# Seven half products for two of three output tiles: a float32 expert layer on one Trainium2 core

## The chip, the core and the metric

The kernel runs on one core of one Trainium2 chip. The metric is the device time of one execution, in microseconds. The profile names the engines PE (TensorE matmul), PEld (TensorE weight load), DVE (VectorE), ACT (ScalarE), POOL (GpSimd) and SP (SyncE).

## The reference

A recurrent attention block feeds a mixture of experts with a hierarchical gate; all inputs and outputs are float32.

```python
# attention: q, k, v, f_logit are (B, H, S, D) = (4, 8, 768, 48)
f = 1.0 / (1.0 + np.exp(-f_logit))
for t in range(S):
    state = f[:, :, t, :, None] * state + np.einsum('bhd,bhe->bhde', k[:, :, t], v[:, :, t])
    y[:, :, t] = np.einsum('bhd,bhde->bhe', q[:, :, t], state)
# x = y as (B*S, H*D) = (3072, 384); G = 4 groups of Eg = 4 experts, F = 1024
g_logits = x @ w_group;  g_idx = argmax(g_logits);  g_w = softmax(g_logits)[g_idx]
for g in range(G):
    xg = x[g_idx == g];  e_logits = xg @ w_expert[g]
    e_idx = argmax(e_logits);  e_w = softmax(e_logits)[e_idx]
    for e in range(Eg):
        h = np.maximum(xg[e_idx == e] @ w1[g, e], 0.0)       # (tokens, 384) @ (384, 1024)
        ye = h @ w2[g, e]                                    # (tokens, 1024) @ (1024, 384)
        out[rows of these tokens] = (g_w * e_w)[:, None] * ye
```

## The kernel before

The first part of the kernel computes attention in chunks of 128 tokens, routes every token to one of 16 experts, and writes the token rows to `x_dram` in DRAM, with the token's gate weight and number behind the 384 features. The experts are ranked by their number of tokens. The second part, which the change is about, runs sixteen expert passes, one for each entry of `PLACES`. Two experts have had their first 128 tokens computed early; what is left of them makes passes 0 and 15, of 128 columns. Passes 1 to 14 are wide: one expert each, with 230, 222, 214, 212, 208, 204, 200, 196, 193, 191, 189, 186, 182 and 174 columns (`WIDTHS`), one column for each token that the pass has room for.

A wide pass goes through these steps:

- `fetch` (L393): GpSimd gathers the token rows (`xg`) by an indirect DMA, three passes ahead. `load_weights` (L381) issues the DMAs of w1 and w2 on SyncE's queue, 1536 KB each, also three passes ahead, as buffers come free.
- `square_in` (L415): 16 transposes of VectorE turn the rows into features by tokens (`xe`). One such instruction turns 32x32 squares of 32 partitions, with 192 or 96 elements each, and writes them to the other 32 partitions where they belong.
- `up` (L439, L440): the first layer. 8 output tiles of 128 features, three products each (a 128x128 block of w1 as the stationary operand, all tokens of the pass moving), two tiles to a PSUM bank, and ScalarE's Relu behind each of the four banks, into `h`.
- `down` (L475, L476): the second layer, turned: three output tiles `m` of 128 features, each the sum of 8 products in one bank (block of w2 stationary, `h` moving), copied by ScalarE into `yT`.
- `square_out` (L422): 16 transposes of VectorE turn `yT` back to token rows `yr`.
- `scaled` and `put` (L447, L450): ScalarE multiplies two blocks of rows by the gate weight into `yt`, and GpSimd scatters them to the output.

In float32 each product is two matmul instructions and two weight loads in the trace. `manual_schedule` holds TensorE, VectorE, ScalarE and SyncE to the order in which the program is written, so the order of the loop is the order of each engine's queue. Iteration n of the loop writes: `square_out` of pass n-1, `square_in` of pass n+2, `up` of pass n+1, `scaled` of pass n-1, `down` of pass n, and the weight loads of pass n+3. So the first layer of the next pass stands on TensorE before the second layer of this pass, and VectorE turns the last pass's output and a later pass's input beside it. In iteration 14 no first layer is left there; that of pass 15 comes after the loop, followed by `turn_out` of pass 14 (transposes on TensorE) and the row-wise second layer of pass 15 (`down_rows`, L460).

PSUM has eight banks in rotation (tag `bank`). After iteration 2, `beyond` computes a table on VectorE of what the passes had no room for (L340 to L372); after iteration 3, `weakest` and `flags` reduce the decays, with one transpose on TensorE (L869). With these inputs the branch that they decide is not taken.

Of the kernel before, what the change touches and what calls it, by code (L numbers as in the profile page):

```python
# [10 lines left out]
FP32 = mybir.dt.float32  # L11
# [4 lines left out]
OP = mybir.AluOpType  # L16
AX = mybir.AxisListType.X
ET = mybir.EngineType
P = 128
SQ = 32  # L20
# [3 lines left out]
def kernel(  # L24
# [12 lines left out]
    nc = tc.nc  # L37
    B, H, S, D = q.shape
    N, DM = out.shape
# [8 lines left out]
    KO = DM // P  # L48
    FO = F // P
    NL = G + GE  # L50
    WIDE = 2 * P
# [28 lines left out]
    def bank(shape, name):  # L80
        return ps.tile(shape, FP32, tag="bank", name=name)
# [253 lines left out]
    def beyond(all_, sb):  # L335

        def tmp(shape, name):
            return sb.tile(shape, FP32, tag=name, bufs=1, name=name)

        SHP = (P, NOV, GE)  # L340
        from_ = tmp([P, GE], "from")
        if all_:
            nc.vector.memset(from_, 0.0)
        else:
            wide = tmp([P, GE, GE], "wide")
            nc.vector.tensor_tensor(wide, order, own.unsqueeze(2).broadcast_to((P, GE, GE)), OP.mult)
            nc.vector.reduce_sum(out=from_, in_=wide.rearrange("p n e -> p e n"), axis=AX)
        nc.vector.tensor_tensor(from_, from_, base, OP.add)
        total = tmp([P, GE], "total")
        nc.vector.tensor_tensor(total, run, from_, OP.subtract)  # L350
        more = tmp([P, GE, NT], "more")
        nc.vector.tensor_tensor(more, total.unsqueeze(2).broadcast_to((P, GE, NT)), steps.unsqueeze(1).broadcast_to((P, GE, NT)), OP.is_gt)
        nb = tmp([P, GE], "nb")
        nc.vector.reduce_sum(out=nb, in_=more, axis=AX)
        end = tmp([P, GE], "end")
        nc.vector.tensor_tensor_scan(end, unit, nb, 0.0, OP.mult, OP.add)
        nc.vector.tensor_copy(b_end, end[0:1, GE - 1:GE])
        beg = tmp([P, GE], "beg")
        nc.vector.tensor_tensor(beg, end, nb, OP.subtract)
        bl = blocks.unsqueeze(2).broadcast_to(SHP)  # L360
        passed = tmp(list(SHP), "passed")
        nc.vector.tensor_tensor(passed, bl, end.unsqueeze(1).broadcast_to(SHP), OP.is_ge)
        be = tmp([P, NOV], "be")
        nc.vector.reduce_sum(out=be, in_=passed, axis=AX)
        nc.vector.tensor_scalar(b_expert, be[0:1], float(GE - 1), None, OP.min)
        mine = tmp(list(SHP), "minb")
        nc.vector.tensor_tensor(mine, bl, beg.unsqueeze(1).broadcast_to(SHP), OP.is_ge)
        nc.vector.tensor_tensor(mine, mine, passed, OP.subtract)
        off = tmp([P, GE], "off")
# [32 lines left out]
    def squares(w, turn):  # L402


        for k_ in range(P // SQ):
            n = sum(j * P + k_ * SQ < w["n"] for j, m in w["blocks"])
            for g in range(P // SQ):
                turn(n, k_, slice(k_ * SQ, (k_ + 1) * SQ), g, slice(g * SQ, (g + 1) * SQ))

    def square_in(w):  # L410

        w["xT"] = room(w, KO, "xe")
        x = w["x"][:, :, 0:DM].rearrange("p j (o g c) -> p j g o c", o=KO, c=SQ)
        xT = w["xT_full"].rearrange("p o (j k c) -> p j k o c", j=2, c=SQ)
        squares(w, lambda n, k_, rk, g, rg: nc.vector.transpose(out=xT[rg, 0:n, k_], in_=x[rk, 0:n, g]))  # L415

    def square_out(w):

        w["rows"] = w["pool"].tile([P, 2, DM], FP32, tag="yr", name="yr")
        y = w["rows"].rearrange("p j (o g c) -> p j g o c", o=KO, c=SQ)  # L420
        yT = w["yT_full"].rearrange("p o (j k c) -> p j k o c", j=2, c=SQ)
        squares(w, lambda n, k_, rk, g, rg: nc.vector.transpose(out=y[rk, 0:n, g], in_=yT[rg, 0:n, k_]))  # L422

    def turn_in(w):
        w["xT"] = room(w, KO, "xe")
# [6 lines left out]
    def up(w, w1):  # L432
        n = w["n"]
        w["h"] = h = room(w, FO, "h")
        for f in range(0, FO, 2):
            hp = bank([P, 2, n], "hp")
            for o in range(2):
                for ko in range(KO):
                    nc.tensor.matmul(hp[:, o, :], lhsT=w1[:, ko, (f + o) * P:(f + o + 1) * P], rhs=w["xT"][:, ko, :], start=(ko == 0), stop=(ko == KO - 1))  # L439
            nc.scalar.activation(h[:, f:f + 2, :], hp, AF.Relu)  # L440
            yield
# [14 lines left out]
    def down_rows(w, w2):  # L456

        yp = bank([P, DM], "yo")
        for fo in range(FO):
            nc.tensor.matmul(yp, lhsT=w["h"][:, fo, :], rhs=w2[:, fo, :], start=(fo == 0), stop=(fo == FO - 1))  # L460
            if fo == FO - 4:
                yield
        put(w, 0, P, yp)

    def down(w, w2):
        n = w["n"]
        if n == P:
            for _ in down_rows(w, w2):
                pass
            return  # L470
        w["yT"] = w["yT_full"][:, :, 0:n]
        for m in range(KO):
            yp = bank([P, n], "yo")
            for fo in range(FO):
                nc.tensor.matmul(yp, lhsT=w2[:, fo, m * P:(m + 1) * P], rhs=w["h"][:, fo, :], start=(fo == 0), stop=(fo == FO - 1))  # L475
            nc.scalar.copy(w["yT"][:, m, :], yp)  # L476

    def scaled(w, settle=False):
        if w["n"] > P:
# [39 lines left out]
    with ExitStack() as fast:  # L519
        sb = fast.enter_context(tc.tile_pool(name="sb", bufs=2))  # L520
        fp = fast.enter_context(tc.tile_pool(name="fp", bufs=1))

        def kept(shape, name):
            return fp.tile(shape, FP32, tag=name, name=name)
# [258 lines left out]
        first, routes = [], []  # L783
# [99 lines left out]
    ws = {n: pass_of(n) for n in range(3)}  # L883
    ahead = {n: load_weights(wq if n % 3 == 1 else wp, who[0:1, PLACES[n]:PLACES[n] + 1]) for n in range(1, 2)}
    ahead[0] = weights[0]

    def const_out(i):

        t = mo.tile([P, KO, WIDE], FP32, tag=f"yT{i}", bufs=1, name=f"yT{i}")
        nc.gpsimd.memset(t[:, :, P:WIDE], 0.0)  # L890
        return t

    def run_up(n):
        for _ in up(ws[n], ahead[n][0]):
            pass

    outs = [const_out(i) for i in range(2)]
    turn_in(ws[0])
    for _ in first[0]:
# [4 lines left out]
    turn_in(ws[1])  # L904
    for _ in opening:
        pass
    for n in range(GE - 1):
# [5 lines left out]
        past, coming = ws.pop(n - 1, None), ws.get(n + 2)  # L913
        if past and past["n"] > P:
            square_out(past)
        if coming and coming["n"] > P:
            square_in(coming)
        if n + 2 < GE:
            run_up(n + 1)
        if past:  # L920

            scaled(past, n == GE - 3)
        if coming and coming["n"] == P:
            turn_in(coming)
        w["yT_full"] = outs[n % 2]
        down(w, ahead.pop(n)[1])
        if n + 3 < GE:
            ahead[n + 3] = load_weights(wq if n % 3 == 1 else wp, who[0:1, PLACES[n + 3]:PLACES[n + 3] + 1])
        if n == 2:
            with tc.tile_pool(name="tb", bufs=1) as tb:  # L930
                beyond(False, tb)
        if n == 3:
            weakest()
            flags()

# [10 lines left out]
    def scan():  # L946

        sb = slow.enter_context(tc.tile_pool(name="sb2", bufs=2))
        y_dram = dp.tile([B * HP, S, 2 * D], FP32, name="y_dram")
        with tc.For_i(0, B * HP, 1) as i:  # L950
            tT = {}
            for nm, src in (("f", f_logit), ("q", q), ("k", k), ("v", v)):
                t = sb.tile([P, NC, 2, DP], FP32, tag="nat", name="nat")
# [15 lines left out]
            yp = [bank([P, HC, 2, D], "yp") for _ in range(2)]  # L969
# [19 lines left out]
        for c in range(NC):  # L989
            lgs = sb.tile([P, B, NL], FP32, tag="lgs2", name="lgs2")  # L990
            for b in range(B):
                x = sb.tile([P, HP, 2, DP], FP32, tag="x2", name="x2")
# [9 lines left out]
                xT = sb.tile([P, HP, P], FP32, tag="x2T", name="x2T")  # L1002
# [7 lines left out]
        beyond(True, sb)  # L1010


    more = nc.values_load(both[0:1, 1:2], min_val=0, max_val=1, skip_runtime_bounds_check_because="the result of a comparison")
    with tc.If(more > 0), ExitStack() as late:
# [3 lines left out]
        mo = late.enter_context(tc.tile_pool(name="mo2", bufs=2))  # L1018
        last = nc.values_load(b_end[0:1, 0:1], min_val=0, max_val=NOV, skip_runtime_bounds_check_because="a count of blocks that N bounds")
        with tc.For_i(0, last, 1) as i:  # L1020
            w1, w2 = load_weights(wp, b_expert[0:1, bass.ds(i, 1)])
# [4 lines left out]
            tb = bank([P, 2], "tb2")  # L1026
# [4 lines left out]
            ts = mo.tile([P, 2], FP32, tag="ts", name="ts")  # L1031
# [3 lines left out]
            w = fetch(ep, row, P, late=True)  # L1035
# [32 lines left out]
```

## Time and profile before

| what | value |
|---|---|
| median of 14 runs | 421.12 us (420.17 to 422.84) |
| the profiled execution | 421.87 us, of which the profile's span is 420.1 us |
| granted TensorE clock, mean | 0.994 |
| TensorE busy, weight loads busy | 408.9 us, 376.4 us |
| VectorE, ScalarE, GpSimd busy | 266.8, 156.8, 83.2 us |
| attention and routing | up to about 149 us of the span |
| passes 1 to 14 | 185 to 404 us of the span |
| second layer of the wide passes (L475) | 672 matmuls, 115.8 us busy |
| output transposes (L422) | 208 instructions, 70.5 us busy |

Busy time counts the time in which an engine had at least one instruction under way; a matmul's end is modelled, and matmuls overlap, so the time from one start to the next says more than one matmul's length. A row's last part names what ended the engine's idle time before it. Line numbers are those of the kernel before.

### The profile page before, as it was taken

The page shows a single profiled execution, that of the slowest core. Times are in us where ns is not written, and L with a number is a line of the kernel's source. Part 1 is how long each engine was busy: PE and PEld are TensorE (multiplying, and loading weights), DVE is VectorE, ACT ScalarE, POOL GpSimd, SP SyncE. Part 2 cuts the span into 40 slices and gives each one's busy share as a digit, 9 for nine tenths or more (in the row PEclk, how much of TensorE's full clock was granted, in tenths as well). Part 3 has the DMA queues.
Part 4 walks back from the last instruction along what each step waited for, and adds up shares of the span by engine and source line. Part 5 has one row for each costly group of instructions (what it writes and reads, how often), then busy time and mean ns, then how long its engine had stood idle before and what let it go on. Part 6 is the DMA issues. An engine that isn't in the chain of part 4 may idle for free.

```text
span 420.1 us, 10066 instructions
## 1 busy us (share of the span) xinstructions
PE 408.9 (97%) x4047; PEld 376.4 (90%) x4047; DVE 266.8 (64%) x778; ACT 156.8 (37%) x353; POOL 83.2 (20%) x127
## 2 busy tenths in 40 slices
PE   8999999999999998999999999999999999999995
PEld 3888888888877966879999999999999999999992
DVE  5666878788886810550599785495685695594240
ACT  6777776767554311211122122231231231231220
POOL 4000010101012166001021331312222221110230
PEclk9999999999999999899999999999999999999999
DMA  9999997878999469937548385595685785585010
GB/s 178 204 201 217 191 177 146 153 140 162 309 335 394 124 235 354 379 92 290 166 165 292 111 321 193 202 324 144 246 316 143 276 300 196 219 318 161 27 46 25
DMA packets 132145, 88.98 MB, mean 212 GB/s; under 512 B 102582, under 2 KB 122748, under 8 KB 132090
## 3 DMA queue, kind: packets, MB, share of 16 engines
q1 hardware_dynamic: 125666, 75.50, 61.7%
q0 software_dynamic: 5792, 11.92, 9.3%
q10 hardware_dynamic: 632, 0.83, 0.6%
q8 instruction: 34, 0.56, 0.5%
q14 instruction: 21, 0.17, 0.1%
HBM read 78.71 MB, written 9.83 MB: 211 GB/s over the span
## 4 chain that ended last, share of the span: by engine, by line
PE 47%; issue 30%; DMA 7%; POOL 6%; DVE 4%; another core or an unknown queue 2%; ACT 1%; POOLq 1%; DVEq 1%
PE hp L439 11%; PE yo L475 6%; DMA out_dram<-yt,xg 6%; PE ap L659 5%; PE y L701 5%; POOL out_dram L450 4%; PE cs L600 4%; PE yo L460 2%; PE x_ps L742 2%; POOL xg L393 2%; PE tr_k L634 2%; PE tr_q L634 2%; PE ds L676 2%; PE y L697 2%
## 5 line engine op out<-in xcount | busy, mean ns | idle before, releaser
L439 PE MATMUL hp<-xe,w 128*128 128x128 f32 (+14 forms) x864 | 141.3, 323 | 2.6 <-issue 1.9
L439 PEld LDWEIGHTS hp<-xe,w 128*128 128x128 f32 x864 | 137.5, 192 | 4.5 <-issue 2.5
L475 PE MATMUL yo<-h,w 128*128 128x230 f32 (+13 forms) x672 | 115.8, 333 | 0.0
L422 DVE STREAM_TRANSPOSE yr<-yT 32x192 f32<-32x192 f32 (+1 forms) x208 | 70.5, 339 | 70.4 <-ACT yT L476 67.8
L475 PEld LDWEIGHTS yo<-h,w 128*128 128x128 f32 x672 | 113.7, 190 | 0.2
L415 DVE STREAM_TRANSPOSE xe<-xg 32x192 f32<-32x192 f32 (+1 forms) x208 | 69.7, 335 | 8.7 <-PE hp L439 5.7
L440 ACT ACTIVATE h<-hp 128x256 f32<-128x256 f32 (+14 forms) x72 | 34.2, 478 | 109.2 <-PE hp L439 100.2
L450 POOL DMA_INDIRECT out_dram<-yt,xg x32 | 34.4, 1076 | 156.5 <-ACT yt L447 150.9
L476 ACT COPY yT<-yo 128x230 f32<-128x230 f32 (+13 forms) x42 | 13.5, 325 | 80.5 <-PE yo L475 80.5
L393 POOL DMA_INDIRECT xg<-x_dram,rows_p x30 | 29.6, 987 | 50.8 <-DMA out_dram<-yt,xg 28.4
L662 DVE TENSOR_TENSOR am<-ap,tri 128x512 f32<-128x512 f32 x48 | 29.8, 682 | 12.7 <-PE ap L659 10.6
L659 PE MATMUL ap<-Tq,Tk 48*64 48x128 f32 x768 | 24.8, 273 | 0.6 <-issue 0.6
L701 PE MATMUL y<-am,v 128*64 128x128 f32 x384 | 24.2, 276 | 0.2
L701 PEld LDWEIGHTS y<-am,v 128*64 128x64 f32 x384 | 20.9, 137 | 3.2 <-DVE am L662 1.6
L659 PEld LDWEIGHTS ap<-Tq,Tk 48*64 48x64 f32 x768 | 21.1, 133 | 2.9 <-issue 2.4
L460 PE MATMUL yo<-w,h 128*128 128x384 f32 x64 | 21.3, 486 | 0.0
L600 PE MATMUL cs<-ld_f,tri 128*128 128x384 f32 x48 | 18.6, 506 | 0.1
L460 PEld LDWEIGHTS yo<-w,h 128*128 128x128 f32 x64 | 11.9, 190 | 7.4
L447 ACT ACTIVATE yt<-yr,xg 128x384 f32<-128x384 f32 (+13 forms) x26 | 14.4, 604 | 5.4 <-DVE yr L422 5.4
L607 POOL DMA_DIRECT2D ends<-eq x10 | 5.4, 541 | 55.2 <-ACT eq L601 55.2
L430 DVE COPY xe<-xg_ps 128x384 f32<-128x384 f32 (+1 forms) x4 | 2.1, 535 | 20.5 <-remote 9.7
L704 ACT COPY xT<-y 128x512 f32<-128x512 f32 x24 | 13.4, 581 | 4.4 <-PE y L701 4.3
(173 smaller groups left out, 381.9 us busy)
## 6 DMA issues: line engine op xcount, KB each, us to landing
w<-in_moe_w_dram SPq DMA_DIRECT2D x34, 1536.0 KB, 7.3
qh<-in_q_dram SPq DMA_DIRECT2D x12, 384.0 KB, 4.6
ld_k<-in_k_dram SPq DMA_DIRECT2D x12, 384.0 KB, 5.7
v<-in_v_dram SPq DMA_DIRECT2D x12, 384.0 KB, 7.1
ld_f<-in_f_logit_dram SPq DMA_DIRECT2D x11, 384.0 KB, 6.1
x_dram<-x_kept SPq DMA_DIRECT2D x2, 1536.0 KB
x_dram<-x POOLq DMA_DIRECT2D x2, 384.0 KB
x_dram<-x ACTq DMA_DIRECT2D x2, 384.0 KB
```

The costliest lines, as they stand in the source:

```text
L393: nc.gpsimd.indirect_dma_start(out=w["x"][:, j, :], out_offset=None, in_=x_dram[0:1 + top, :], in_offset=bass.IndirectOffsetOnAxis(ap=rows ...
L415: squares(w, lambda n, k_, rk, g, rg: nc.vector.transpose(out=xT[rg, 0:n, k_], in_=x[rk, 0:n, g]))
L422: squares(w, lambda n, k_, rk, g, rg: nc.vector.transpose(out=y[rk, 0:n, g], in_=yT[rg, 0:n, k_]))
L439: nc.tensor.matmul(hp[:, o, :], lhsT=w1[:, ko, (f + o) * P:(f + o + 1) * P], rhs=w["xT"][:, ko, :], start=(ko == 0), stop=(ko == KO - 1))
L440: nc.scalar.activation(h[:, f:f + 2, :], hp, AF.Relu)
L450: sent = nc.gpsimd.indirect_dma_start(out=out, out_offset=bass.IndirectOffsetOnAxis(ap=w["x"][0:m, j, DM + 1:RW].bitcast(U32), axis=0), in ...
L460: nc.tensor.matmul(yp, lhsT=w["h"][:, fo, :], rhs=w2[:, fo, :], start=(fo == 0), stop=(fo == FO - 1))
L475: nc.tensor.matmul(yp, lhsT=w2[:, fo, m * P:(m + 1) * P], rhs=w["h"][:, fo, :], start=(fo == 0), stop=(fo == FO - 1))
L600: nc.tensor.matmul(cs.rearrange("t h d -> t (h d)"), lhsT=tri, rhs=nl[:, b], start=True, stop=True)
L659: nc.tensor.matmul(ap[r][half, a, :], lhsT=w["Tk"][rows, b, a, half], rhs=w["Tq"][rows, b, a, :], start=True, stop=True)
L662: nc.vector.tensor_tensor(am[:, r], ap[r], tri.unsqueeze(1).broadcast_to((P, HP, P)), OP.mult)
L701: nc.tensor.matmul(ys[b][DP * h:DP * h + DP, a, :], lhsT=w["v"][:, b, 2 * a + (b ^ h), :], rhs=w["am"][b][:, b ^ h, a, :], start=(c == 0 a ...
```

## The change

Of the three output tiles of a wide pass's second layer, the first two are no longer computed as 16 full products. They form a 2x2 block matrix with the two halves of the 1024 inner features (A11, A21 for tile 0, A12, A22 for tile 1), and `h` is cut into 2x2 blocks by the same halves and by two halves of the tokens (B11 and so on). Winograd's form of Strassen's scheme gives the four output blocks by seven products of half the columns, each of four 128x128 blocks, instead of eight, with sums and differences in float32. VectorE makes four sums of w2 for each pass (`sums_of`, 128x512 each, a pass ahead) and four differences of `h` (`differences`); the products accumulate in three banks that ScalarE and VectorE read between products (m1, u2, u3), and five VectorE additions and two ScalarE copies finish the blocks. The third tile stays as it was, with its 8 full products.

The output turn becomes one VectorE transpose over all 128 partitions (`yz`), and 16 ScalarE copies (`moved`) bring its squares to their places in `yr`, four behind each Relu of the next pass's first layer. The 16 transposes of the input are issued in groups: 8 before the sums, 4 and 4 inside the second layer. `beyond` is cut into pieces, one at the end of each of iterations 2 to 6, and `weakest` and `flags` move from iteration 3 to iteration 6.

```diff
     def square_out(w):
+        nb = (w["n"] + SQ - 1) // SQ
+        z = w["pool"].tile([P, KO, WIDE // SQ, SQ], FP32, tag="yz", bufs=1, name="yz")
+        nc.vector.transpose(out=z[:, :, 0:nb], in_=w["yT_full"].rearrange("p o (b c) -> p o b c", c=SQ)[:, :, 0:nb])
+        w["turned"] = z
+
+    def moved(w):
         w["rows"] = w["pool"].tile([P, 2, DM], FP32, tag="yr", name="yr")
         y = w["rows"].rearrange("p j (o g c) -> p j g o c", o=KO, c=SQ)
-        yT = w["yT_full"].rearrange("p o (j k c) -> p j k o c", j=2, c=SQ)
-        squares(w, lambda n, k_, rk, g, rg: nc.vector.transpose(out=y[rk, 0:n, g], in_=yT[rg, 0:n, k_]))
+        z = w["turned"].rearrange("p o (j k) c -> p j k o c", j=2)
+        moves = []
+        squares(w, lambda n, k_, rk, g, rg: moves.append((y[rk, 0:n, g], z[rg, 0:n, k_])))
+        for i, (to, from_) in enumerate(moves):
+            nc.scalar.copy(to, from_)
+            if i % 4 == 3:
+                yield
...
-        w["yT"] = w["yT_full"][:, :, 0:n]
-        for m in range(KO):
-            yp = bank([P, n], "yo")
-            for fo in range(FO):
-                nc.tensor.matmul(yp, lhsT=w2[:, fo, m * P:(m + 1) * P], rhs=w["h"][:, fo, :], start=(fo == 0), stop=(fo == FO - 1))
-            nc.scalar.copy(w["yT"][:, m, :], yp)
+    def sums_of(w2):
+        t = mo.tile([P, 4, FO // 2, P], FP32, tag="ws", bufs=2, name="ws")
+        a11, a12 = (w2[:, k_ * FO // 2:(k_ + 1) * FO // 2, 0:P] for k_ in range(2))
+        a21, a22 = (w2[:, k_ * FO // 2:(k_ + 1) * FO // 2, P:2 * P] for k_ in range(2))
+        for out_, x, y, op in ((0, a21, a22, OP.add), (1, t[:, 0], a11, OP.subtract), (2, a11, a21, OP.subtract), (3, a12, t[:, 1], OP.subtract)):
+            nc.vector.tensor_tensor(t[:, out_], x, y, op)
+        return t
...
+    def differences(w):
+        half = (w["n"] + 1) // 2
+        (b11, b12), (b21, b22) = halves_of(w)
+        t = mo.tile([P, 4, FO // 2, WIDE // 2], FP32, tag="hs", bufs=1, name="hs")[:, :, :, 0:half]
+        for out_, x, y in ((0, b12, b11), (1, b22, t[:, 0]), (2, b22, b12), (3, b21, t[:, 1])):
+            nc.vector.tensor_tensor(t[:, out_], x, y, OP.subtract)
+        w["ts"] = t
+
+    def down_halves(w, w2, sums, between):
...
+        def product(bank_, l, r, first):
+            for f in range(FO // 2):
+                nc.tensor.matmul(bank_, lhsT=l[:, f, :], rhs=r[:, f, :], start=first and f == 0, stop=f == FO // 2 - 1, skip_group_check=True)
+
+        r1, r3, r2 = (bank([P, half], "yo") for _ in range(3))
+        m1, u2, u3 = (kept(nm) for nm in ("m1", "u2", "u3"))
+        product(r1, a(0, 0), b11, True)
+        nc.scalar.copy(m1, r1)
+        product(r3, sums[:, 1], t[:, 1], True)
+        nc.vector.tensor_tensor(u2, r3, m1, OP.add)
+        product(r2, sums[:, 0], t[:, 0], True)
+        product(r1, a(1, 0), b21, False)
+        nc.scalar.copy(yT[:, 0, 0:half], r1)
+        between(4)
+        product(r3, sums[:, 2], t[:, 2], False)
+        nc.vector.tensor_tensor(u3, r3, m1, OP.add)
+        nc.vector.tensor_tensor(yT[:, 1, half:n], r2[:, skip:half], u3[:, skip:half], OP.add)
+        between(4)
+        yp = bank([P, n], "yo")
+        for fo in range(FO):
+            nc.tensor.matmul(yp, lhsT=w2[:, fo, 2 * P:DM], rhs=w["h"][:, fo, :], start=(fo == 0), stop=(fo == FO - 1))
+        nc.scalar.copy(yT[:, 2, :], yp)
+        product(r2, sums[:, 3], b22, False)
+        nc.vector.tensor_tensor(yT[:, 0, half:n], r2[:, skip:half], u2[:, skip:half], OP.add)
+        product(r3, a(1, 1), t[:, 3], False)
+        nc.vector.tensor_tensor(yT[:, 1, 0:half], r3, m1, OP.add)
...
         if past and past["n"] > P:
             square_out(past)
-        if coming and coming["n"] > P:
-            square_in(coming)
+            moves = moved(past)
+        if w["n"] > P:
+            differences(w)
+        between = lambda k_: [next(turns, None) for _ in range(k_)]
+        between(8)
         if n + 2 < GE:
-            run_up(n + 1)
+            sums[n + 1] = sums_of(ahead[n + 1][1])
+            for _ in up(ws[n + 1], ahead[n + 1][0]):
+                next(moves, None)
+        for _ in moves:
+            pass
         if past:
             scaled(past, n == GE - 3)
...
+        if w["n"] > P:
+            down_halves(w, ahead.pop(n)[1], sums.pop(n), between)
+        else:
+            down(w, ahead.pop(n)[1])
+        for _ in turns:
+            pass
+        for g in spare:
+            next(g, None)
...
-        if n == 3:
+        if n == 6:
             weakest()
             flags()
```

More of the change, by code (lines that the diff above doesn't have):

```diff
@@ L362, in beyond @@
         nc.vector.tensor_tensor(passed, bl, end.unsqueeze(1).broadcast_to(SHP), OP.is_ge)
+        yield
         be = tmp([P, NOV], "be")
@@ L368, in beyond @@
         nc.vector.tensor_tensor(mine, mine, passed, OP.subtract)
+        yield
         off = tmp([P, GE], "off")
@@ L414, in square_in @@
         xT = w["xT_full"].rearrange("p o (j k c) -> p j k o c", j=2, c=SQ)
-        squares(w, lambda n, k_, rk, g, rg: nc.vector.transpose(out=xT[rg, 0:n, k_], in_=x[rk, 0:n, g]))
-    def square_out(w):
+        turns = []
+        squares(w, lambda n, k_, rk, g, rg: turns.append((xT[rg, 0:n, k_], x[rk, 0:n, g])))
+        for to, from_ in turns:
+            nc.vector.transpose(out=to, in_=from_)
+            yield
+    def square_out(w):
+        nb = (w["n"] + SQ - 1) // SQ
[3 more added lines that the diff above has]
+    def moved(w):
         w["rows"] = w["pool"].tile([P, 2, DM], FP32, tag="yr", name="yr")
         y = w["rows"].rearrange("p j (o g c) -> p j g o c", o=KO, c=SQ)
-        yT = w["yT_full"].rearrange("p o (j k c) -> p j k o c", j=2, c=SQ)
-        squares(w, lambda n, k_, rk, g, rg: nc.vector.transpose(out=y[rk, 0:n, g], in_=yT[rg, 0:n, k_]))
+        z = w["turned"].rearrange("p o (j k) c -> p j k o c", j=2)
[4 more added lines that the diff above has]
+            if i % 4 == 3:
+                yield
     def turn_in(w):
@@ L465, in down @@
     def down(w, w2):
-        n = w["n"]
[L467 to L470, printed above, removed]
-        w["yT"] = w["yT_full"][:, :, 0:n]
-        for m in range(KO):
-            yp = bank([P, n], "yo")
-            for fo in range(FO):
-                nc.tensor.matmul(yp, lhsT=w2[:, fo, m * P:(m + 1) * P], rhs=w["h"][:, fo, :], start=(fo == 0), stop=(fo == FO - 1))
-            nc.scalar.copy(w["yT"][:, m, :], yp)
+        for _ in down_rows(w, w2):
+            pass
@@ new lines, in sums_of, with halves_of @@
+    def sums_of(w2):
[5 more added lines that the diff above has]
+        return t
+    def halves_of(w):
+        n = w["n"]
+        half = (n + 1) // 2
+        return [[w["h"][:, k_ * FO // 2:(k_ + 1) * FO // 2, j * (n - half):j * (n - half) + half] for j in range(2)] for k_ in range(2)]
@@ new lines, in differences, with kept @@
+    def differences(w):
[6 more added lines that the diff above has]
+    def down_halves(w, w2, sums, between):
+        n = w["n"]
+        half = (n + 1) // 2
+        skip = 2 * half - n
+        (b11, b12), (b21, b22) = halves_of(w)
+        t = w["ts"]
+        a = lambda k_, m: w2[:, k_ * FO // 2:(k_ + 1) * FO // 2, m * P:(m + 1) * P]
+        yT = w["yT"] = w["yT_full"][:, :, 0:n]
+        def kept(name):
+            return mo.tile([P, WIDE // 2], FP32, tag=name, bufs=1, name=name)[:, 0:half]
+        def product(bank_, l, r, first):
[23 more added lines that the diff above has]
+        nc.vector.tensor_tensor(yT[:, 1, 0:half], r3, m1, OP.add)
@@ L895, in run_up @@
             pass
+    tb = main.enter_context(tc.tile_pool(name="tb", bufs=1))
     outs = [const_out(i) for i in range(2)]
@@ L906 @@
         pass
+    sums, spare = {}, []
     for n in range(GE - 1):
@@ L913 @@
         past, coming = ws.pop(n - 1, None), ws.get(n + 2)
+        wide_in = bool(coming) and coming["n"] > P
+        turns = square_in(coming) if wide_in else iter(())
+        moves = iter(())
         if past and past["n"] > P:
             square_out(past)
-        if coming and coming["n"] > P:
-            square_in(coming)
-        if n + 2 < GE:
-            run_up(n + 1)
+            moves = moved(past)
[3 more added lines that the diff above has]
+        between(8)
+        if n + 2 < GE:
+            sums[n + 1] = sums_of(ahead[n + 1][1])
[3 more added lines that the diff above has]
+            pass
         if past:
             scaled(past, n == GE - 3)
-        if coming and coming["n"] == P:
+        if coming and not wide_in:
             turn_in(coming)
         w["yT_full"] = outs[n % 2]
-        down(w, ahead.pop(n)[1])
+        if n == 2:
+            spare.append(beyond(False, tb))
+        if w["n"] > P:
[3 more added lines that the diff above has]
+        for _ in turns:
+            pass
+        for g in spare:
+            next(g, None)
         if n + 3 < GE:
             ahead[n + 3] = load_weights(wq if n % 3 == 1 else wp, who[0:1, PLACES[n + 3]:PLACES[n + 3] + 1])
-        if n == 2:
-            with tc.tile_pool(name="tb", bufs=1) as tb:
-                beyond(False, tb)
-        if n == 3:
+        if n == 6:
             weakest()
@@ L1009, in scan @@
                 pass
-        beyond(True, sb)
+        for _ in beyond(True, sb):
+            pass
     more = nc.values_load(both[0:1, 1:2], min_val=0, max_val=1, skip_runtime_bounds_check_because="the result of a comparison")
```

## The prediction

> **What bounds the kernel now.** I read the page's busy rows and 40 slices first, then the windows cut at the passes, then the timeline of one pass, then the groups kept apart by shape.
>
> ```profile
> PE 408.9 (97%) x4047; PEld 376.4 (90%) x4047; DVE 266.8 (64%) x778; ACT 156.8 (37%) x353; POOL 83.2 (20%) x127
> ...
> PE   8999999999999998999999999999999999999995
> PEld 3888888888877966879999999999999999999992
> ```
>
> From slice 17 on both rows of TensorE stand at 9: matmuls and weight loads are back to back. The windows (one expert pass each, then the last half pass) say it exactly.
>
> ```profile
> core 0: us, PE busy (x) PEld busy (x) DVE busy (x) ACT busy (x) POOL busy (x), PEclk, DMA share, GB/s
> ...
> 203.40:221.10 17.70, 17.70 (x98) 17.70 (x98) 16.27 (x45) 4.16 (x9) 3.34 (x4) 1.00 0.57 196
> ...
> 272.20:288.60 16.40, 16.40 (x98) 16.40 (x97) 11.03 (x32) 4.00 (x9) 3.39 (x5) 1.00 0.67 230
> ...
> 396.60:403.70 7.10, 7.10 (x50) 7.10 (x50) 5.12 (x16) 1.44 (x4) 0.24 (x1) 1.00 0.00 0
> ```
>
> TensorE never stops here and its granted clock is 1.00, so every nanosecond of TensorE that is added or removed in the passes is on the path, and there is no idle time to win back. VectorE is busy for 11 of 16.4 us, ScalarE for 4.
>
> ```profile
> 143.14 5.44 PEld L439 LDWEIGHTS hp<-xe,w 128*128 128x128 f32 x48
> 143.17 5.60 PE L439 MATMUL hp<-xe,w 128*128 128x128 f32 x48
> ...
> 148.50 0.30 PEld L460 LDWEIGHTS yo<-w,h 128*128 128x128 f32 x2
> ...
> 351.40 7.60 PEld L439 LDWEIGHTS hp<-xe,w 128*128 128x128 f32 x48
> 351.56 7.72 PE L439 MATMUL hp<-xe,w 128*128 128x186 f32 x48
> 353.71 0.48 ACT L440 ACTIVATE h<-hp 128x372 f32<-128x372 f32 x1 [1.58 <-PE hp L439]
> 359.32 0.48 ACT L440 ACTIVATE h<-hp 128x372 f32<-128x372 f32 x1 [1.41 <-PE hp L439]
> ...
> 402.57 1.12 ACT L447 ACTIVATE yt<-yr,xg 128x384 f32<-128x384 f32 x2 [5.43 <-DVE yr L422]
> ```
>
> Columns: start, length, engine, line, tile, count. A layer's 24 float32 products are 48 matmuls with 48 loads, two of each per product. At 186 columns 48 matmuls run from 351.56 to the next group at 359.12, 157.5 ns each. Over the fourteen widths the same reading gives width/1.2 + 2.5 ns (230: 194, 174: 147). At 128 columns that formula says 109 ns, and the row shows (5.44 - 0.19)/47 = 112. That is where loads set the pace: a load lasts 0.19, and two loads that nothing held up (the row at 148.50, ahead of 384-column matmuls of 322 ns) took 0.30, so they started 0.11 apart. I find no two such loads closer than 108 ns.
>
> ```profile
> L440 ACT ACTIVATE h<-hp 128x400 f32<-128x400 f32 x4 | 2.0, 504 | 6.2 <-PE hp L439 6.2
> ...
> L476 ACT COPY yT<-yo 128x200 f32<-128x200 f32 x3 | 1.0, 325 | 6.0 <-PE yo L475 6.0
> ```
>
> ```profile
> L422 DVE STREAM_TRANSPOSE yr<-yT 32x192 f32<-32x192 f32 x144 | 53.1, 369 | 69.6 <-ACT yT L476 67.8
> ...
> L662 DVE TENSOR_TENSOR am<-ap,tri 128x512 f32<-128x512 f32 x48 | 29.8, 682 | 12.7 <-PE ap L659 10.6 <-remote 2.1
> ```
>
> In the groups kept apart by shape (count, then busy us, mean ns) these price the added work: ScalarE 0.84 ns an element plus 0.165 us, the next one starting 0.10 before the last ends (the two L447 of 0.60 in 1.12); VectorE adds 0.68 us for 512 elements and 0.57 for 390; a square transpose 0.37.
>
> **The change, part by part: TensorE.** Per wide pass it removes 2 x 8 products, 32 matmuls at width/1.2 + 2.5 ns. The fourteen widths sum to 2801, so 32 x (2801/1.2 + 14 x 2.5) = 75.8 us. It adds 7 x 4 half products, 56 matmuls and 56 full weight loads for 87 to 115 columns. By columns these would cost 75 to 98 ns each; by loads 108 to 112. The nearest row is the 128-column one, and a load does not get shorter because fewer columns follow it, so I take 111.5: 14 x 56 x 0.1115 = 87.4 us. Net +11.6 us (ends +8.9 at 108, +14.4 at 115). The third output tile and the first layer are unchanged.
>
> The page "TensorE: Matmul & The Clock Gate" of the Trainium skill speaks on both sides. Its section "Back-to-back issue gap" prices a warm matmul at N/2.4 + 2.5 ns; read for two array passes per instruction that is the trace's own width/1.2 + 2.5, would put a mean half product at 86 ns, and would make this term -8.4. Its section "LDWEIGHTS (loading the stationary operand)" says that a load costs its columns over 1.2, whatever follows: an estimated 107 ns, and +7.8. It adds under "Weight-path perf modes" that the fast load is not for float32. The 112 ns at 128 columns agrees with the second.
>
> **VectorE.** Sixteen output transposes (16 x 0.38 = 6.1 us) become one of 128 partitions x 672 elements; from 0.27 us for 96 and 0.37 for 192 elements it is 0.86. Added: four differences (0.60 each with the 34 ns between dependent operations), four sums of w2 (0.71 each), five small adds (0.28). In order from the end of a pass: last add 0.48, transpose 0.89, differences 2.40, eight input transposes 3.06, sums 2.86: 9.7 us beside a first layer of some 8.0, so VectorE is free 1.7 us after the second layer starts, before it is wanted. The sums need w2 a pass earlier than before; the load queue's rows have each w2 issued two passes ahead and landed in about 7.3 us, which leaves about ten; without them the sums would hold up VectorE, and u2 and the next input behind them. Nothing moves on the queues of SyncE and GpSimd but the scatters, about as late in their pass as now.
>
> The extra table work of `beyond` (L362 to L372: 0.8 us an operation) is cut into pieces of 1.5, 2.5, 2.7 and 2.3 us that stand between a pass's last add and the next transpose. The last three push the chain above past the point where u2 must have read its bank: 0.6 + 0.9 + 0.6 = 2.1 us of TensorE in passes 4 to 6 (ends 0 and 5). `weakest` now stands straight behind the last add of pass 6, and its transpose on TensorE waits for add and reduction: 0.85 us; now it is found ready.
>
> **ScalarE, and the wait it makes.** Sixteen copies of 192 or 96 elements, four behind each Relu; behind the last four come two scalings (L447) and only then the copy m1, which TensorE needs before its fourth product may write bank r1 again. No row has a copy from 32 partitions of SBUF; between 192 elements from PSUM (L747, 325 ns) and the same with 25 ns more (L447 costs 602 from SBUF against 580 from PSUM) I take the longer, 0.26 us a step with the overlap and 0.18 for the short ones. From the start T0 of the second layer: Relu starts at 0.20 (the row at 359.32 against 359.12), steps 0.40; four short copies 0.70, ending 0.10 later; the scaling waits for them, 0.06; two scalings 1.00; m1 0.25; signal 0.06: ready at 2.77. TensorE gets there at 24 x 0.1115 = 2.68. So 0.1 us in each of ten passes, 0.5 in pass 2, whose copies are all long: 1.5 us (ends: none if a copy costs 0.03 less; 9 to 11 if ScalarE steps without overlap). Queued behind m1 on ScalarE are only copies of the same layer; u2 on VectorE waits for it too, inside the 0.89 us of the fourth product.
>
> **The last wide pass (14).** No first layer lies between 13 and 14 (the row 396.60 to 403.70). Today two second layers run on without a gap. Now the third product needs two differences behind a 0.76 us transpose that follows pass 13's last add: 0.5 + 0.8 + 1.2 = 2.5 us against 0.89: 1.6 of waiting. Then m1 stands behind sixteen copies in a row (8 x 0.26 + 8 x 0.18 = 3.4) and two scalings, and comes 2.0 us late. Together 3.6 us (ends 2 and 6), all on the path, since only the last expert follows.
>
> **Sum.** 11.6 + 1.5 + 2.1 + 0.85 + 3.6 = 19.6 us. Against the profiled execution (span 420.1, time 421.87) that is 441.5. That run is 0.75 above the median of the runs, so against 421.12 I forecast 440.7. The measurement tells about 0.2%, 0.8 us, from no change.
>
> **Rivals.**
> 1. *Half products at column price, waits covered: faster.* If loads hide, 56 x (1402/1.2 + 35) = 67.4 us replaces 75.8: -8.4, less up to 4.4 at the tail and `weakest`: 413 to 417. It decides once loads can start under some 86 ns apart. Against it: the 108 ns floor and the 112 at 128 columns. Chance 0.03.
> 2. *Loads hide, but m1 does not.* TensorE then wants r1 back at 24 x 0.086 = 2.06 us, not 2.68, and waits 0.6 more in twelve passes (7.4), which gives back most of the 8.4; the other 8.0 us of waits stay: +7 to +8, 428 to 429. Chance 0.06.
> 3. *ScalarE or VectorE becomes the bound.* If copies run without the 0.10 overlap or cost 0.1 us more, m1 comes 0.9 us late per pass instead of 0.1: +25 to +28, 446 to 450; at 0.2 more per copy ScalarE no longer keeps up with the first layer (+41). For it: no row has this copy. Against it: L447 reads SBUF and overlaps. Chance 0.2.
> The forecast keeps 0.71, with its own range 434 to 447. That the halves are not what TensorE gets is not open: the order of its instructions has the 28 half products per pass.
>
> **Numbers.** 430 to 455 leaves out the first rival, half of the second and the far end of the third, plus a little of the forecast. Faster by over 0.2% is the first rival with a little more, 0.04; within 0.2% only a mixture of cases, 0.02; slower 0.94.
>
> **What the next profile would show.** Right: half products 108 to 112 ns apart whatever their width, weight loads without gaps there; small waits of TensorE for m1 ahead of the fourth product; a hole of some 3.6 us in pass 14. Wrong if half products step by their columns (75 to 98 ns), if TensorE waits over 0.5 us in ordinary passes, or if the copies show over 0.4 us each.

## The result and the profile after

| kernel | median | ratio to the kernel before |
|---|---|---|
| before | 421.75 us (47 runs) | 1 |
| changed | 451.13 us (10 runs, 448.78 to 453.66) | 1.070 (95% interval 1.068 to 1.072) |

The change makes the kernel 7% slower. The profiled execution took 450.35 us, with a span of 448.5 us, 28.4 us more than the span before.

The busy rows and the clock row of the changed kernel's profile:

```profile
PE 426.2 (95%) x4383; PEld 391.7 (87%) x4383; DVE 288.7 (64%) x765; ACT 220.8 (49%) x561; POOL 82.9 (18%) x127
...
PEclk9999999999999998999999999999999999999888
```

There are 336 more matmuls and as many more loads, ScalarE has 64 us more work, VectorE 22, and the clock row now ends in three 8s. Windows of the changed kernel: a stretch at pass 2, one at pass 6 with the wait for `weakest` in it, then passes 13 and 14.

```profile
core 0: us, PE busy (x) PEld busy (x) DVE busy (x) ACT busy (x) POOL busy (x), PEclk, DMA share, GB/s
204.00:222.00 18.00, 17.32 (x114) 17.14 (x114) 12.29 (x30) 9.42 (x25) 2.54 (x3) 1.00 0.57 193
286.00:303.00 17.00, 15.84 (x113) 15.48 (x112) 12.68 (x37) 7.54 (x23) 3.92 (x4) 1.00 0.60 205
399.50:415.80 16.30, 16.30 (x126) 16.17 (x124) 6.96 (x15) 8.45 (x25) 2.26 (x2) 1.00 0.38 118
415.80:432.00 16.20, 11.44 (x75) 11.15 (x74) 3.81 (x10) 6.71 (x21) 1.95 (x2) 0.79 0.05 17
```

TensorE, which had no gap at all in these stretches before, now has one in each of the ordinary passes, none that this row shows in pass 13, and two of nearly 5 us together in pass 14, where the granted clock is 0.79 as well. One ordinary pass in the timeline of the changed kernel (pass 7, 200 columns; start, length, engine, line, tile, count, and in brackets the engine's idle time and what ended it):

```profile
304.77 1.03 PE L526 MATMUL yo<-h,w 128*128 128x100 f32 x8
304.97 0.50 ACT L459 ACTIVATE h<-hp 128x392 f32<-128x392 f32 x1
305.48 1.11 ACT L439 COPY yr<-yz 32x96 f32<-32x96 f32 x4
305.64 1.95 PE L526 MATMUL yo<-hs,ws 128*128 128x100 f32 x16
306.62 1.12 ACT L466 ACTIVATE yt<-yr,xg 128x384 f32<-128x384 f32 x2
307.65 0.22 ACT L531 COPY m<-yo 128x100 f32<-128x100 f32 x1
307.92 1.14 PE L526 MATMUL yo<-h,w 128*128 128x100 f32 x8 [0.33 <-ACT m L531]
308.89 1.06 PE L526 MATMUL yo<-hs,ws 128*128 128x100 f32 x8
309.79 2.90 PE L544 MATMUL yo<-h,w 128*128 128x200 f32 x16
```

Two things are to be seen. Groups of 8 half-width matmuls start 0.87 to 0.90 us apart wherever nothing is waited for (305.64 less 304.77 is 0.87, 309.79 less 308.89 is 0.90; 308.89 less 307.92 is 0.97, as the load catches up behind a wait): about 0.111 each, where 100 columns would be worth 0.086. And ScalarE goes without a break from Relu through four short copies and two scalings to m1, and TensorE waits for m1. From the last start of the third product to the first of the fourth are 0.61 us instead of 0.11. The waits list of the changed kernel (total us, times, longest) names the same pair:

```profile
PE yo L526 <- ACT m L531: 8.4, 12, 3.4
```

Read from start to start, the time of the changed trace over the one before divides like this:

| where | us | by the prediction |
|---|---|---|
| half products at load pace: 14 x 56 matmuls in 87.1 us for 75.8 | 11.3 | 11.6 |
| TensorE late at the fourth product, passes 2 to 13 | 7.0 | 1.5 for m1 and 2.1 for u2 |
| `weakest` behind pass 6 | 0.8 | 0.85 |
| pass 14, two waits (1.55 and 3.54) | 5.1 | 3.6 |
| pass 14, slow matmuls after the second wait | 2.5 | - |
| the rest, in pieces of under 0.1 us a group: 0.4 ahead of the passes, about 1 in the fourth products of passes 2 to 13, whose loads catch up behind the wait (0.97 for 0.89) | 1.7 | - |

Pass 14 in the timeline of the changed kernel:

```profile
416.45 0.78 DVE L428 STREAM_TRANSPOSE yz<-yT 128x576 f32<-128x576 f32 x1
417.26 5.11 ACT L439 COPY yr<-yz 32x192 f32<-32x192 f32 x16 [2.61 <-DVE yz L428]
418.33 1.99 PE L526 MATMUL yo<-hs,ws 128*128 128x87 f32 x16 [1.39 <-DVE hs L508]
422.41 1.12 ACT L466 ACTIVATE yt<-yr,xg 128x384 f32<-128x384 f32 x2
423.43 0.21 ACT L531 COPY m<-yo 128x87 f32<-128x87 f32 x1
423.69 2.01 PE L526 MATMUL yo<-h,w 128*128 128x87 f32 x8 [3.38 <-ACT m L531]
425.49 1.91 PE L526 MATMUL yo<-hs,ws 128*128 128x87 f32 x8
427.20 3.23 PE L544 MATMUL yo<-h,w 128*128 128x174 f32 x16
```

The sixteen copies take 5.11 us, TensorE stands 3.38 us for m1, and then eight half-width matmuls last 2.01 where they last 1.06 elsewhere. The granted clock fell inside that stop, 1.4 us after its start (two windows, columns as above; the clock is the third number from the end):

```profile
420.30:421.70 1.40, 0.02 (x1) 0.00 (x0) 0.00 (x0) 1.34 (x6) 0.00 (x0) 1.00 0.00 0
421.80:428.50 6.70, 4.81 (x21) 4.81 (x22) 0.75 (x3) 2.02 (x7) 1.95 (x2) 0.50 0.11 39
```

### The profile page after: what moved, and what is told of

Read it like the earlier page. It is cut to its first block, busy times and chain, and to the rows that moved or that the text cites. A ratio compares the mean times of both kernels' runs of the same rounds, so it can differ in the third digit from the quotient of the medians.

```text
span 448.5 us, 10901 instructions
## 1 busy us (share of the span) xinstructions
PE 426.2 (95%) x4383; PEld 391.7 (87%) x4383; DVE 288.7 (64%) x765; ACT 220.8 (49%) x561; POOL 82.9 (18%) x127
## 4 chain that ended last, share of the span: by engine, by line
PE 49%; issue 25%; ACT 7%; DVE 6%; DMA 5%; POOL 4%; another core or an unknown queue 2%; POOLq 1%; DVEq 1%; SPq 0%
PE hp L458 12%; PE yo L526 6%; PE yo L544 5%; ACT yr L439 4%; PE ap L732 4%; PE y L774 4%; PE cs L673 3%; POOL out_dram L469 2%; PE yo L479 2%; PE x_ps L815 2%; DMA out_dram<-yt,xg 2%; PE tr_k L707 2%; PE ds L749 2%; PE tr_q L707 2%
## 5 line engine op out<-in xcount | busy, mean ns | idle before, releaser
L439 ACT COPY yr<-yz 32x192 f32<-32x192 f32 (+1 forms) x208 | 67.3, 323 | 7.2 <-DVE yz L428 5.0
L526 PE MATMUL yo<-hs,ws 128*128 128x115 f32 (+13 forms) x336 | 43.0, 279 | 1.4 <-DVE hs L508 1.4
L526 PEld LDWEIGHTS yo<-hs,ws 128*128 128x128 f32 x336 | 40.6, 195 | 1.5 <-issue 1.5
L544 PE MATMUL yo<-h,w 128*128 128x230 f32 (+13 forms) x224 | 41.2, 338 | 0.0
L526 PE MATMUL yo<-h,w 128*128 128x115 f32 (+13 forms) x224 | 31.1, 283 | 8.4 <-ACT m L531 8.4
L544 PEld LDWEIGHTS yo<-h,w 128*128 128x128 f32 x224 | 38.1, 194 | 0.1
L526 PEld LDWEIGHTS yo<-h,w 128*128 128x128 f32 x224 | 28.7, 196 | 10.6 <-ACT m L531 10.4
L545 ACT COPY yT<-yo 128x230 f32<-128x230 f32 (+13 forms) x14 | 4.6, 327 | 48.9 <-PE yo L544 48.9
L533 DVE TENSOR_TENSOR u<-yo,m 128x115 f32<-128x115 f32 (+13 forms) x14 | 3.7, 263 | 31.0 <-ACT m L531 31.0
L547 DVE TENSOR_TENSOR yT<-yo,u 128x115 f32<-128x115 f32 (+13 forms) x14 | 3.7, 262 | 29.2 <-PE yo L526 29.2
```

The costliest lines, as they stand in the source:

```text
L439: nc.scalar.copy(to, from_)
L526: nc.tensor.matmul(bank_, lhsT=l[:, f, :], rhs=r[:, f, :], start=first and f == 0, stop=f == FO // 2 - 1, skip_group_check=True)
L544: nc.tensor.matmul(yp, lhsT=w2[:, fo, 2 * P:DM], rhs=w["h"][:, fo, :], start=(fo == 0), stop=(fo == FO - 1))
```

## The experiments

The theory was: the second layer got slower by the pace of weight loads, by a copy (m1) that stands behind other work on ScalarE, and by pass 14, and by nothing else. The rivals were that half products go by their columns and everything is waits, that the ScalarE copies cost time by themselves, and that VectorE stands close behind ScalarE. Each run went beside the kernel before on the same chip (416.8 or 421.1 us there), so ratios are compared.

### Half products of 128 columns

```diff
-        half = (n + 1) // 2
+        half = P
```

(in all three places where the half is computed)

> The changed kernel, with both halves of the tokens widened to 128 columns (they overlap in the middle, so 13 to 41 columns per product are computed twice). The number of half products and of weight loads stays. If loads set the pace of the half products, 128 columns cost what 87 to 115 do: matmuls 109 to 112 ns apart, second layers as long as in the changed kernel, total within 2 us of it (449 to 453 us; a little more than zero, because VectorE's differences and additions grow by some 0.1 us each). If columns set the pace, 784 matmuls get on average 28 columns more at 1/1.2 ns each: 18 us more, 469 us.

Measured: 443.95 us, ratio 1.066 (1.060 to 1.071), against 1.070 (1.068 to 1.072) for the changed kernel. The same two groups of products, first in the changed kernel, then here (count, busy us, mean ns):

```profile
L526 PE MATMUL yo<-hs,w 128*128 128x115 f32 (+13 forms) x112 | 14.8, 275 | 0.0
...
L526 PE MATMUL yo<-h,ws 128*128 128x115 f32 (+13 forms) x112 | 14.4, 272 | 0.0
```

```profile
L526 PE MATMUL yo<-hs,w 128*128 128x128 f32 x112 | 14.8, 275 | 0.0
L526 PE MATMUL yo<-h,ws 128*128 128x128 f32 x112 | 14.8, 274 | 0.0
```

The busy time of these groups is the same, and so is their pace: groups of eight start 0.89 us apart here too. 784 matmuls with 28 columns more on average are free (the two ratios' intervals overlap). Column price is out: it asked for 18 us.

### The kernel before with tiles 0 and 1 in two halves

```diff
-            for fo in range(FO):
-                nc.tensor.matmul(yp, lhsT=..., rhs=w["h"][:, fo, :], ...)
+            cut = (n + 1) // 2
+            for part in ((slice(0, cut), slice(cut, n)) if m < 2 else (slice(0, n),)):
+                for fo in range(FO):
+                    nc.tensor.matmul(yp[:, part], lhsT=..., rhs=w["h"][:, fo, part], ...)
```

> The kernel before, and of the change only the narrow matmuls: output tiles 0 and 1 of each wide pass are computed in two halves of the tokens, 64 half-width matmuls in place of 32, with no sums, no differences, no seven products and the old turn on VectorE. Load pace: 14 x 64 x 0.111 = 99.3 us for 75.8, so 23.5 us more than before: 445 us, ratio 1.056. Column price: only 64 x 14 times the 2.5 ns per matmul, 1.1 us more than before: 423 us, ratio 1.003.

Measured: 440.67 us, ratio 1.056 (1.051 to 1.061). In its timeline one pass:

```profile
263.66 10.12 PE L477 MATMUL yo<-h,w 128*128 128x104 f32 x80
273.62 8.28 PE L439 MATMUL hp<-xe,w 128*128 128x200 f32 x48
```

The second layer of 208 columns takes 9.96 us from start to start instead of 8.44. The arithmetic is the same and no engine but TensorE has anything more to do: the narrow matmuls alone cost 23.9 us, with no wait.

### The change without its seven products

```diff
-            down_halves(w, ahead.pop(n)[1], sums.pop(n), between)
+            down_plain(w, ahead.pop(n)[1])
```

`down_plain` is the wide branch of the old `down`; the sums and differences are left out too.

> The changed kernel without its seven products: no sums, no differences, all three output tiles by full products; the outputs are still turned whole by VectorE and moved by 16 copies of ScalarE, and the table work is still cut up and moved. If the loss comes from the half products and from waits that exist only because the second layer needs ScalarE and VectorE between its products, this is the kernel before again, plus at most the 0.8 us that TensorE waits for the moved reduction: 421 to 423 us, ratio 1.00. If the copies on ScalarE cost time by themselves (Relu behind them, banks released late), it keeps what is left of the loss beside the load pace: about 440 us.

Measured: 416.73 us, ratio 1.000 (0.998 to 1.002). Turning the outputs whole and moving them on ScalarE costs nothing and gains nothing while nobody waits for ScalarE. Its windows (passes of 222 and 204 columns, the columns of the table as above):

```profile
207.00:224.70 17.70, 17.70 (x98) 17.70 (x97) 8.39 (x23) 9.69 (x26) 4.07 (x4) 1.00 0.56 194
274.50:290.90 16.40, 16.40 (x99) 16.31 (x98) 7.10 (x23) 9.22 (x26) 3.91 (x4) 1.00 0.64 217
```

VectorE is down from 11.03 to 7.10 us in the second stretch, ScalarE up from 4.00 to 9.22, and TensorE is full as before. Nor does the moved `weakest` make TensorE wait here, since VectorE has no last add ahead of it.

### m1 ahead of the scalings

```diff
         nc.scalar.copy(m1, r1)
+        late()
```

`late` issues the two scalings (`scaled`), which no longer stand ahead of the second layer.

> The changed kernel with one move on ScalarE: the two scalings of the last pass's rows are issued behind the copy m1 and no longer ahead of it. If m1 is late because ScalarE's queue is full of work that nobody waits for, m1 comes 1.0 us earlier: the wait ahead of the fourth product (0.5 to 1.1 us in passes 2 to 12) goes to zero, pass 14 loses 1 of its 3.5 us, and the kernel gains 7 to 9 us: 443 us. If VectorE (u2 behind the sums of w2) is close behind, the wait only changes its owner and the gain is under 3 us: 449 us.

Measured: 441.31 us, ratio 1.050 (1.046 to 1.053), 2.0 points or 8.6 us less than the change. The fourth product waits nowhere in passes 1 to 13 but once (0.17 us in pass 5, where a table piece precedes). VectorE was not close behind. The microsecond that was expected in pass 14 did not come: the wait for m1 there falls from 3.38 to 0.85 us, but the granted clock drops already behind the first stop, of 1.39 us, and the pass takes 15.7 us for 16.1. Two windows of this run, one inside that stop and one from 0.2 us after its end (columns as above):

```profile
407.00:408.50 1.50, 0.18 (x2) 0.03 (x1) 1.47 (x4) 0.97 (x3) 0.00 (x0) 1.00 0.00 0
408.80:418.90 10.10, 9.25 (x41) 9.02 (x41) 1.23 (x5) 5.28 (x17) 1.95 (x2) 0.50 0.08 27
```

### Pass 14 by full products

```diff
+        if n == GE - 2:
+            down_plain(w, ahead.pop(n)[1])
```

The differences and the sums of w2 for pass 14 are left out too.

> The changed kernel, with pass 14 alone by full products. The trace shows two idle stretches of TensorE in pass 14 (1.6 and 3.5 us) and after them matmuls at about half the pace for some 5 us. If the slow matmuls follow from the idle stretch, everything goes: 16.1 us of second layer become 7.1, gain 9 us, 442 us. If they have another cause, only the waits and the load pace go: gain 6.6 us, and the matmuls after pass 13 stay slow.

Measured: 440.16 us, ratio 1.048 (1.044 to 1.052), 2.25 points or 9.5 us less. Its windows for passes 13 and 14, columns as above:

```profile
398.40:414.70 16.30, 16.30 (x126) 16.17 (x124) 4.46 (x11) 8.44 (x25) 2.26 (x2) 1.00 0.37 118
414.70:421.80 7.10, 7.10 (x50) 7.10 (x49) 1.03 (x2) 5.53 (x18) 0.00 (x0) 1.00 0.01 3
```

7.1 us for 16.2, at a clock of 1.00 for 0.79. So the slow matmuls belonged to the stops.

### All waits out, half products kept

The two edits above together, the table pieces issued behind the third tile's copy, and the reduction of `weakest` issued ahead of the second layer of pass 6.

> The changed kernel with every wait that its trace shows taken out and the half products kept: the two scalings of the last pass's rows stand behind the copy m1 on ScalarE, pass 14 uses full products, the table pieces stand in VectorE's free time inside the second layer, and the reduction is made before its transpose is wanted. If load pace is what remains, it loses only that: some 10.5 us over the kernel before (13 passes x 56 x 0.111 us against 32 matmuls by columns), 432 us, ratio 1.025. If there is a further cost that the trace hides, it stays above 436. If half products went by columns it would be faster than before: 414 us.

Measured: 428.14 us, ratio 1.028 (1.022 to 1.033): 11.3 us over the kernel before, where thirteen passes at load pace account for 9.8. The other 1.5 is less than the spread of its four runs (426.22 to 429.55). One pass of its timeline (pass 7 again):

```profile
293.74 1.10 ACT L439 COPY yr<-yz 32x96 f32<-32x96 f32 x4
293.90 1.95 PE L528 MATMUL yo<-hs,ws 128*128 128x100 f32 x16
294.87 0.24 ACT L533 COPY m<-yo 128x100 f32<-128x100 f32 x1
295.14 1.12 ACT L466 ACTIVATE yt<-yr,xg 128x384 f32<-128x384 f32 x2
295.69 1.06 PE L528 MATMUL yo<-h,w 128*128 128x100 f32 x8
```

m1 is done at 295.11, 0.58 us ahead of the matmul that needs it, and that row has no idle time in brackets. This is the best form of the change that I ran, and the kernel before beats it.

### 256 columns, with and without the half products

```diff
-    WIDTHS = (230, 222, 214, 212, 208, 204, 200, 196, 193, 191, 189, 186, 182, 174)
+    WIDTHS = (256,) * 14
```

> The kernel before with all fourteen wide passes given 256 columns (3584 for 2801; the added ones hold no tokens). It is the partner of the next run. Every wide matmul goes by its columns: 783 more columns x 96 matmuls a pass x 1/1.2 ns = 62.6 us more than the kernel before, ratio 1.15.

> The changed kernel without its waits (scalings behind m1, pass 14 by full products, table pieces and reduction moved), with 256 columns in every wide pass, so that a half product moves 128. If a half product costs the larger of its weight load (0.111 us) and its columns, 56 of them cost 6.2 us against 6.9 for the 32 full matmuls that they replace: 13 x 0.69 = 9 us less than the kernel before with 256 columns, about 0.98 of its time, where with 174 to 230 columns the same form was 2.8% slower. If half products carry a cost of their own beside loads and columns, the sign stays: slower than its partner.

Measured: full products 479.48 us, ratio 1.151 (1.149 to 1.153); half products without waits 471.05 us, ratio 1.130 (1.129 to 1.132). The second is 0.982 of the first, 8.4 us faster. Where a half product moves 128 columns, the scheme pays. A second layer in the timelines of the two, full first:

```profile
274.28 10.52 PE L475 MATMUL yo<-h,w 128*128 128x256 f32 x48
```

```profile
331.06 1.05 PE L528 MATMUL yo<-h,w 128*128 128x128 f32 x8
331.95 1.95 PE L528 MATMUL yo<-hs,ws 128*128 128x128 f32 x16
333.74 1.06 PE L528 MATMUL yo<-h,w 128*128 128x128 f32 x8
334.64 1.06 PE L528 MATMUL yo<-hs,ws 128*128 128x128 f32 x8
335.53 3.62 PE L547 MATMUL yo<-h,w 128*128 128x256 f32 x16
338.99 1.05 PE L528 MATMUL yo<-h,ws 128*128 128x128 f32 x8
339.88 1.06 PE L528 MATMUL yo<-hs,w 128*128 128x128 f32 x8
340.77 0.60 PE L458 MATMUL hp<-xe,w 128*128 128x256 f32 x2
```

From 331.06 to 340.77 are 9.71 us, for 10.36 with full products (284.64 less 274.28).

### The old turn on VectorE, with the seven products

`moved` issues VectorE's 16 square transposes again, in place of the one transpose and the copies.

> The changed kernel with the old turn of the outputs: 16 square transposes of VectorE per pass, no copies on ScalarE. It tells whether the move to ScalarE was needed. VectorE then has 0.5 + 6.1 + 2.4 + 3.1 + 2.9 = 15 us of work in a row before it can read the bank for u2, against a first layer of 8 us: if so, u2 comes 3 to 4 us late in each of twelve passes, m1 no longer late, and the kernel is slower by 35 to 40 us: about 487 us. If the ScalarE copies are the whole of the wait, taking them away gains the 7 us: 444 us.

Measured, in one run: 506.1 us. Its waits list:

```profile
PE yo L522 <- DVE u L529: 33.7, 11, 3.9
```

The wait is where it was expected and of that size; the single time is 19 us above what I expected. Pass 14 waits another 6.1 us for its differences, which the expectation had left out, and the granted clock of this run is 0.929: behind five of the eleven waits for u the next eight matmuls take 2.02 to 2.05 us, where they take 1.13 to 1.15 behind five others. So the stops again cost pace as well, though not by their length alone: behind a wait of 2.50 us the eight are slow at once, behind one of 3.85 they are not. So the move to ScalarE was needed for the half products.

### Why the copies do not overlap

Three forms of the 16 copies: into their own partitions (rows not in place, tile cleared by GpSimd), by an activation instruction, and as one unbroken piece in their own partitions.

> The changed kernel, with each of the 16 copies writing to the 32 partitions that it reads, and GpSimd clearing the tile ahead of them; the rows of the wide passes are therefore not in their places. In the changed kernel a copy of 192 elements is followed by the next 0.357 us later, with no overlap, where two scalings overlap by 0.10. If the overlap is lost because the copy crosses partitions, copies in place step by 0.25 us, the waits for m1 shrink to 0.1 us and the kernel gains 6 to 8 us. If it is lost for another reason (source and target both in SBUF, the pieces of 32 elements), nothing changes: 0.357 us a step.

> The changed kernel, its 16 copies made by an activation instruction (function Copy, scale 1) in place of the copy instruction; same elements, same places. In the trace two scalings (activations from SBUF to SBUF) overlap by 0.10 us and two copies from SBUF do not overlap at all. If the instruction makes the difference, the copies step by 0.25 us, the wait for m1 falls from 0.5 to 0.1 us a pass and the kernel gains 6 to 8 us: 443 us. If not, 0.357 us a step and no change.

> The changed kernel with copies in their own partitions and of one unbroken piece of 192 (or 96) elements, GpSimd clearing the tile ahead of them; the rows of the wide passes are not in their places. If the pieces of 32 elements cost the overlap, a step falls from 0.357 to 0.25 us and the kernel gains 6 to 8 us. If not, nothing changes, and what is left is that the source is in SBUF, or that the copy covers 32 partitions.

Measured: 450.59 us in one run beside 421.07; 446.65 us, ratio 1.072 (1.070 to 1.074); 447.99 us in one run beside 416.81. None helps. Four copies in a row, one line from each timeline in that order:

```profile
299.99 1.44 ACT L440 COPY yr<-yz 32x192 f32<-32x192 f32 x4
```

```profile
296.06 1.48 ACT L439 ACTIVATE yr<-yz 32x192 f32<-32x192 f32 x4
```

```profile
294.90 1.42 ACT L442 COPY yr<-yz 32x192 f32<-32x192 f32 x4
```

Neither crossing partitions nor the kind of instruction nor the pieces of 32 elements takes the overlap away. Nor do the 32 partitions or the source in SBUF by themselves. The first copy of a pass has both, and in all nine passes of the changed kernel in which it waits for nothing else it starts 0.10 us before the Relu ahead of it has ended, here at 299.40 for 299.50:

```profile
299.00 0.50 ACT L459 ACTIVATE h<-hp 128x392 f32<-128x392 f32 x1 [4.39 <-PE hp L458]
299.40 1.42 ACT L439 COPY yr<-yz 32x192 f32<-32x192 f32 x4
```

That first copy reads and writes from partition 0 on, as the instructions ahead of it do. Each of the other fifteen, in all four forms, reads from another partition on than the last instruction ahead that read SBUF, and none of them overlaps. A change of the start partition as the cause fits these rows, but no run changes it alone, so the cause is not shown.

## Why the prediction was right, and where it was off

The measured 451.1 us is slower, as forecast, and lies in the stated 430 to 455, but above the forecast's own range of 434 to 447. One of the prediction's signs of being wrong came: TensorE waited over 0.5 us in four ordinary passes (idle for 0.68, 0.58, 0.91 and 0.56 us in passes 2, 4, 5 and 6). The mechanism was right, one wait was mis-sized, and one cost was missing.

**Direction and bound.** TensorE was full, so what the change did to TensorE set the time. Right: no other part of the change moves the time while TensorE does not wait for it (the run with full products, 1.000). One reading was off without harm: the row of weight loads stands at 9 from slice 19 on, not 17.

**Load pace, +11.6.** Right: 11.3 in the trace, shown three times over, by widening (free), by splitting (+23.9 us alone) and by 256 columns (the sign turns). The section "LDWEIGHTS (loading the stationary operand)" of the Trainium skill's page "TensorE: Matmul & The Clock Gate" prices a load by its own columns, an estimated 107 ns here. The runs agree in that 87 to 128 columns behind the load made no difference; the pace stood at 111 to 112 ns, 4 to 5 above. The page's "Back-to-back issue gap" formula alone, of which that section itself says that it under-counts at small N, would have had the sign wrong.

**The wait for m1, 1.5 us.** This is the term that was mis-sized. It took "0.26 us a step with the overlap" from the row of the scalings. The length of a copy was right (0.348 us in the trace, 25 ns above the copies from PSUM), but the copies, the first of a pass apart, do not overlap with what is ahead of them: 1.42 us for four is 0.357 a step. In ordinary passes the four short copies behind the last Relu start 0.51 us after it instead of 0.40 and take 1.11 us instead of 0.80 (pass 7 above), and m1 therefore came 0.5 us late instead of 0.1. With the same overlap in pass 14 that is 5 of the 10 us by which the forecast of 440.7 is low; slow matmuls in pass 14 and the small pieces make up 4 more. The third rival described just that ("run without the 0.10 overlap") and priced it at 446 to 450; I gave it 0.2. That its price came near the measured time is in part luck: it had m1 0.9 us late a pass, where 0.5 was measured, and no slow matmuls.

**The table pieces, 2.1 us through u2.** The size was half of that (0.74, 1.07 and 0.72 us of wait in passes 4 to 6, some 1.0 more than their neighbours together), and the way is wrong: u2 held nothing up. The pieces delay the whole transpose, that delays the copies, and these delay m1. With m1 ahead of the scalings only 0.17 us of it is left.

**`weakest`, 0.85 us.** Right: 0.77.

**Pass 14, 3.6 us.** The place and both waits were right (1.55 for the differences as forecast 1.6; 3.54 for m1, forecast 2.0, again by the overlap: the sixteen copies took 5.1 us instead of 3.4; the prediction's own steps add up to 3.5). That the granted clock falls to 0.50 there and the matmuls run slow, 2.5 us more, was not in the sum.

**Covers.** The sums of w2 never waited for their load, and VectorE had its work done before u2 was wanted, as worked out; the run with the old turn shows how near that is, since 5 us more of VectorE a pass uncover 3 to 4 us of waiting.

## What to carry to other kernels

Price a matmul by the larger of its weight load and its moving columns before cutting it: here a half product has a floor of 0.111 us per instruction, so seven half products beat eight only from a full width of about 230 columns (56 x 0.111 = 32 x (width/1.2 + 2.5 ns)), and at 256 they did by 1.8% of the kernel. When a PSUM bank must be read between two products, put that read ahead of everything in its engine's queue that nobody waits for; here the order of two instructions was worth 2%. And take an overlap between instructions only from a row of the same instruction on the same kind of operands; a row that is merely near had the length right and the step wrong.

## What the runs showed of the hardware that I had not expected

- ScalarE copies from SBUF of 32 partitions, each starting at another partition than the one ahead, step by 10 ns more than their length (0.357 for 0.348), where the first of a pass, copies from PSUM and scalings of 54 to 128 partitions start 0.10 us before the one ahead has ended.
- Behind the stop of 3.4 us in pass 14 TensorE's matmuls started 0.213 us apart instead of 0.111, and those of 174 columns 0.29 instead of 0.147, for nearly 5 us, with the granted clock at 0.50; by full products, without the stops, they did not. The stop need not be that long: with m1 ahead of the scalings the clock fell behind a stop of 1.39 us. The waits of 0.3 to 0.9 us in passes 2 to 12 left it at 1.00. How much idle time it takes, and within what stretch, these runs do not settle. The same page of the Trainium skill, in its part on the clock gate, puts the half clock behind at least one idle window of about 3.4 us. The stretches at 0.50 behind pass 14's stops last 6.8 us in the changed kernel, 10.2 with m1 ahead and 3.4 with halves of 128 columns, whole numbers of such windows, but in the first two of these runs TensorE had stood for only 1.4 us at a stretch when the clock fell.
